# Bias of the second matmul: from TensorE's sums to additions on GpSimd, and a warm-up in small tiles

## The chip, the cores and the metric

The kernel runs on one core of one Trainium2 chip. The core has five engines with queues of their own: TensorE (PE, matmuls, with its weight loads shown apart as PEld), VectorE (DVE), ScalarE (ACT), GpSimd (POOL) and SyncE (SP, which here only issues DMAs). PE writes to PSUM; DVE and ACT read and write PSUM and SBUF; POOL works on SBUF here. The metric is the time of one execution on the device, in microseconds (us); less is better.

## What is computed

```python
xn = layernorm(x)                                   # x: 2048 x 512
s = A(xn)       # a state space layer: a long convolution of each of 512 channels, with its skip
h = gelu(xn @ w1 + b1)                              # 2048 x 1792
g = silu(h @ w2 + b2)                               # 2048 x 512
out = x + s * g
```

The change concerns `+ b2` alone: the same 512 numbers are added to every row of `h @ w2`.

## The kernel before

The rows of xn are cut into four groups of 512 (index t or v, 0 to 3), each of four blocks of 128 rows (index i). The 1792 columns of h are cut into 14 blocks (f). Every operand of the two large products is split into a high and a low part, and three matmuls (high by high, high by low, low by high) stand for one. The weights do not all fit, so the four groups go through the first seven blocks of h (v = 0 to 3), and then again through the other seven (v = 4 to 7). Between the two passes the sums of a group wait in device memory.

For each pair (v, f): `first_half` makes h before its activation in PSUM, `gate` applies the activation on ACT (tile hf), `gate_high` takes the high part (hh, ACT), `ffn_rest` the low part (hl, DVE), and `second_part` adds the three products with the block of w2 to the sums z of the group, four PSUM tiles of 128 x 512, one for each i.

After the seventh block of the first pass, `z_copy(t, i)` empties the sums into SBUF (tile zo): ACT copies the even ones (L411), DVE takes the odd ones and adds b2 while doing so (L413, with b2b, b2 spread over all 128 rows by one DMA, L443). `z_keep` stores zo (SP, L416). In the second pass `z_load` brings them back (zi, L422), DVE's `z_add` adds the new sums (L451), and ACT applies silu. For the last group `z_last` lets ACT copy the sums and POOL add them (L455, L456).

So for odd i, b2 is added by DVE in the copy. For even i it is put into PSUM by PE: in `second_part`, before the first product of a group, one matmul of a 128 x 128 tile of ones with b2r starts the sum (L292). b2r has b2's high part in row 0 and its low part in row 32 and zeros elsewhere; `bias_load`, `bias_high` and `bias_low` make it and the ones, with two DMAs of POOL's queue, two memsets (DVE), two casts (ACT) and a subtraction of one row (DVE). `bias_load` also makes the tile `one`, on which ACT loads its tables early.

Beside all this, the same engines build the convolution's kernel, in 32 steps s: `gen_phase` (PE, a bf16 matmul into one of two PSUM buffers called ph, L620), `gen_round` (ACT L628 or DVE L630), `gen_wrap` (DVE, L634, the last reader of ph), `gen_size` (POOL, tile mm, L640 to L645), `gen_sin` (ACT), `gen_tables` (DVE, tiles e, L666 to L673, from mm and ra, all in SBUF), and for each two steps `gen_sum` (PE, 64 matmuls of 128 x 32 by 128 x 64, L682, two records each) and `gen_out` (ACT, L693). The split of later weights into high and low parts (`split`) is done by ACT and DVE, three times by POOL (L236).

What runs on an engine runs in the order in which the program issues it. That order is written out by hand: ORDER is a list of about 1250 tokens such as `S.16.0` (second_part of pair 16, block 0) or `Z.6` (gen_size of step 6), each of which calls one of the functions above. The tokens that matter here: `O.t.i` z_copy, `OK.t` z_keep, `ZL.t` z_load, `ZA.t.i` z_add, `Z.s` gen_size, `E.s.n` gen_tables, `R.j` ffn_rest, `S.j.i` second_part, `A.s.h` gen_phase, `Q.j` gen_sum, `WS.f.k` split, `KL` table loads on SP, `BL` bias_low.

After the list follow the convolution's transforms, almost all of them matmuls in tiles smaller than the whole array (L895, L911, L965, L1037), to the end.

Before the list the prologue loads the first rows and normalizes them. While it waits, `warm(n)` keeps PE busy with n matmuls of the identity by itself, 128 x 128 in f32, which the profile shows as two records each: 6 of them, a small transpose, then 17 more.

Of the kernel before, what the change touches and what calls it, by code (L numbers as in the profile page):

```python
# [20 lines left out]
P = 128  # L21
# [12 lines left out]
TB = 4  # L34
# [14 lines left out]
W.2 P.0 P.0 WB.2 WS.1.0 WS.1.1 WS.1.2 W.4 W.3 F.1.0 F.1.1 BL G.0 WS.2.0 P.0 LL.2 LL.3 WS.4.0 H.0 WB.3 WS.2.1  # L49
WS.0.3 G.1 WS.2.2 P.0 W.5 F.2.0 WS.3.0 H.1 P.0 R.0 F.2.1 G.2 WB.5 WB.4 WS.5.0 WS.5.1 WS.3.1 WS.2.3 W.6 S.0.0  # L50
WS.4.1 WS.3.2 R.1 F.3.0 WS.4.2 F.3.1 S.0.1 WS.1.3 G.3 S.0.2 H.2 LS.3.1 S.1.0 LS.2.0 LS.3.0 WS.6.0 H.3 LS.2.1
P.0 LD.0 S.1.1 F.4.0 S.1.2 P.0 P.0 F.4.1 P.1 WS.5.2 P.0 P.0 WB.6 LR.2 P.0 CB S.0.3 F.5.0 KL.0.0 KL.1.0 P.0 G.4
R.2 H.4 F.5.1 S.1.3 S.2.0 LD.1 S.2.1 S.2.2 R.3 LL.5 G.5 P.1 LC.2 S.2.3 TF.2.0 LC.3 WS.3.3.1 WS.6.1 WS.4.3.1
TF.2.1 A.0.0 B.0.0 A.0.1 S.3.0 H.5 LL.4 TH.2.0 TL.2.0 S.3.1 S.3.2 R.4 TH.2.1 TF.3.1 P.0 S.3.3 A.1.0 WS.5.3.1
C.0.0 TL.2.1 WS.6.2 KL.2.0 R.5 LD.3 TH.3.1 TL.3.1 S.4.0 B.0.1 C.0.1 F.6.0 WS.6.3 F.6.1 P.0 B.1.0.1 TF.3.0 G.6
KL.0.1 TH.3.0 KL.3.0 H.6 LS.5.0 S.4.1 N.0.0 C.1.0 A.1.1 KL.1.1 S.4.2 Z.0 B.1.1 LS.5.1 TL.3.0 S.5.0 F.8.0 LD.2
LS.4.0 S.5.1 R.6 N.0.1 S.6.0 LS.4.1 A.2.0 Z.1 C.1.1 S.6.1 F.7.0 S.4.3 A.2.1 N.1.0 S.5.2 F.7.1 N.1.1 F.8.1 LR.4
KL.3.1 BB S.5.3 E.0.0 LC.4 S.6.2 G.7 F.9.0 S.6.3 P.1 E.0.1 E.0.2 G.8 E.1.0 F.9.1 LK.0 F.10.0 E.1.1 A.3.0 O.0.0
H.7 R.7 E.1.2 B.2.0.1 TF.4.0 O.0.2 KL.4.0 KL.2.1 F.10.1 H.8 C.2.0 G.9 Q.0 LK.1 B.2.1 R.8 C.2.1 S.7.0 TF.4.1
S.7.1 Z.3 S.7.2 H.9 R.9 B.3.0.1 N.2.0 LD.4 D A.3.1 TH.4.0 KL.4.1 S.8.0 O.0.1 G.10 S.9.0 Z.2 P.1 U.0 N.2.1  # L60
C.3.0 B.3.1 H.10 O.0.3 S.7.3 UD.0 F.11.0 S.8.1 S.9.1 TL.4.0 E.2.0 S.8.2 TH.4.1 P.1 C.3.1 N.3.0 E.2.1 F.11.1
A.4.0 A.4.1 KL.5.0 LC.5 N.3.1 S.9.2 OK.0 KL.6.0 F.12.0 R.10 B.4.0.1 TL.4.1 F.12.1 E.2.2 E.3.0 S.10.0 P.1 B.4.1
LD.5 S.8.3 Z.4 C.4.0 G.12 C.4.1 S.10.1 E.3.1 TF.5.1 P.1 S.9.3 S.10.2 TF.5.0 KL.5.1 E.3.2 G.11 P.1 TH.5.1 Q.1
TH.5.0 LL.7 A.5.0 LL.6 N.4.0 TL.5.1 S.10.3 A.5.1 H.11 B.5.0 U.1 F.13.0 H.12 TL.5.0 F.13.1 P.1 KL.7.0 R.11
F.14.0 C.5.0 R.12 LS.6.0 N.4.1 F.14.1 P.1 S.11.0 P.2 S.12.0 S.11.1 S.11.2 B.5.1 E.4.0 G.13 H.13 P.1 G.14 C.5.1
A.6.0 F.15.0 E.4.1 S.11.3 N.5.0 F.15.1 P.1 N.5.1 KL.7.1 E.4.2 F.16.0 S.12.1 Z.5 S.12.2 H.14 A.6.1 B.6.0.1 R.13
LS.7.0 S.12.3 A.7.0 S.13.0 KL.6.1 S.13.1 S.13.2 LS.7.1 G.15 E.5.0 C.6.0 E.5.1 E.5.2 P.2 B.6.1.1 B.7.0 R.14
H.15 C.7.0 S.13.3 C.6.1 O.1.0 F.16.1 LS.6.1 F.17.0 Z.7 P.1 F.17.1 O.1.2 S.14.0 N.6.0 R.15 LR.6 S.15.0 G.16
# [95 lines left out]
def kernel(  # L164
# [118 lines left out]
    def second_part(v, f, i):  # L283
# [7 lines left out]
        if rows:  # L291
            PE.matmul(z, ones, b2r, start=True, stop=False)  # L292
# [122 lines left out]
    def z_keep(t):  # L415
        SY.dma_start(za[t].rearrange("i p d -> p i d"), zt[t, "o"])  # L416
# [843 lines left out]
```

## Time and profile before

| | |
|---|---|
| median of 3 runs | 524.7 us (524.53 to 524.74) |
| span of the profiled execution, first to last instruction | 523.6 us |
| what lies around the span, by the median of the runs | 1.1 us |
| records of PE matmuls | 5447 |
| instructions of POOL | 425, 329.8 us busy |

The profiled execution has no time of its own beside its span, so the median of the runs stands for it. A row of the timeline reads: start and length in us, engine, line, operation, output<-inputs, shape, count; in brackets the idle time of the engine before it, and what ended it. A row of a line's or a tile's own view has durations in ns (least/median/most), then the first and last start in us. A matmul's length covers its way through the array and overlaps the next one's: what it costs in a full queue is the step from one start to the next.

### The profile page before, as it was taken

Reading aid. Unit: us, or ns where it says so; the run is one execution under the profiler, and the core shown is the slowest. Engines: PE = TensorE matmul, PEld = TensorE weight load, DVE = VectorE, ACT = ScalarE, POOL = GpSimd, SP = SyncE. Lnnn points to the kernel's source line nnn. Section 1 sums busy time; section 2 is a strip of 40 time slices with the busy share of each in tenths; the row PEclk is TensorE's granted clock in tenths of the full one; section 3 lists DMA queues with packets and bytes.
Section 4 is the critical chain, followed back from the end, with each engine's and each line's share of the span. In section 5 each row is a group of like instructions: output and inputs, shape, how many; then the busy total and the mean of one; then the engine's idle time right before and its main releaser. Section 6 shows DMA issues by size and latency. Waiting matters only on the chain.

```text
span 523.6 us, 13568 instructions
## 1 busy us (share of the span) xinstructions
PE 505.3 (97%) x5447; PEld 371.7 (71%) x5447; DVE 456.7 (87%) x698; ACT 357.6 (68%) x518; POOL 329.8 (63%) x425
## 2 busy tenths in 40 slices
PE   7999999999999999999999999999999999999993
PEld 7777777777777777777778777777754565656671
DVE  6999989997889979999999899799767878697885
ACT  4838976788688889968779997888824333334340
POOL 6748598664857397975874845684336433947732
PEclk9999999999999999999999999999999999999998
DMA  8757965239266839150067376148469979364694
GB/s 228 188 160 231 297 177 172 69 98 297 74 174 192 255 121 327 41 201 33 32 172 206 114 205 176 59 71 149 134 199 371 173 170 146 98 147 97 147 241 99
DMA packets 106751, 85.63 MB, mean 164 GB/s; under 512 B 41646, under 2 KB 82624, under 8 KB 106688
## 3 DMA queue, kind: packets, MB, share of 16 engines
q1 hardware_dynamic: 96400, 65.80, 48.4%
q0 software_dynamic: 8960, 17.97, 11.4%
q10 hardware_dynamic: 1328, 0.98, 0.7%
q8 instruction: 43, 0.70, 0.6%
q14 instruction: 20, 0.16, 0.1%
HBM read 51.18 MB, written 33.55 MB: 162 GB/s over the span
## 4 chain that ended last, share of the span: by engine, by line
PE 70%; DVE 17%; ACT 4%; POOL 2%; issue 2%; DMA 2%; SPq 0%; ACTq 0%; POOLq 0%; DVEq 0%
PE s L911 12%; PE z L293 7%; PE z L294 7%; PE z L295 7%; PE f L251 7%; PE f L253 7%; PE f L252 7%; PE sa_p L965 6%; PE kg L682 4%; PE s L895 3%; DMA x<-in_A_u_dram 2%; PE ph L620 2%; DVE hl L280 2%; DVE x L368 2%; DVE e L670 1%
## 5 line engine op out<-in xcount | busy, mean ns | idle before, releaser
L643 POOL TENSOR_TENSOR mm<-mm,rc 128x32 f32<-128x32 f32 (+4 forms) x150 | 108.1, 721 | 11.8
L293 PE MATMUL z<-w2h,hh 128*128 128x512 f32 x224 | 97.7, 436 | 0.0
L251 PE MATMUL f<-xh,w1h 128*128 128x512 f32 x220 | 90.5, 411 | 1.0 <-DVE xl L400 1.0
L295 PE MATMUL z<-w2h,hl 128*128 128x512 f32 x224 | 88.4, 395 | 0.8 <-DVE hl L280 0.8
L294 PE MATMUL z<-w2l,hh 128*128 128x512 f32 x224 | 88.6, 396 | 0.0
L252 PE MATMUL f<-xl,w1h 128*128 128x512 f32 x220 | 86.9, 395 | 0.8 <-DVE xl L400 0.8
L253 PE MATMUL f<-xh,w1l 128*128 128x512 f32 x220 | 86.9, 395 | 0.4 <-DVE w1l L236 0.4
L911 PE MATMUL s<-X,mc 128*64 128x256 f32 x512 | 64.2, 393 | 0.4 <-DVE X L903 0.4
L640 POOL COPY mm<-rc 128x32 f32<-128x32 f32 x30 | 19.5, 652 | 64.9 <-DVE e L673 42.6
L930 DVE TENSOR_TENSOR t<-s,uh 128x512 f32<-128x512 f32 x62 | 39.7, 669 | 20.8 <-ACT uh L922 20.8
L911 PEld LDWEIGHTS s<-X,mc 128*64 128x64 f32 x512 | 34.1, 134 | 31.6 <-issue 5.9
L666 DVE TENSOR_TENSOR e<-mm,ra 128x1024 f32<-128x1024 f32 x32 | 43.6, 1366 | 13.6 <-ACT ra L654 8.7
L268 ACT ACTIVATE hf<-f,b1s 128x512 f32<-128x512 f32 x56 | 38.1, 689 | 19.5 <-PE f L253 11.6
L293 PEld LDWEIGHTS z<-w2h,hh 128*128 128x128 f32 x224 | 42.5, 190 | 12.7 <-issue 3.9
L280 DVE TENSOR_TENSOR hl<-hf,hh 128x512 fp32r<-128x512 f32 x56 | 49.5, 890 | 2.1 <-ACT hh L274 2.0
L922 ACT COPY uh<-s 128x512 f32<-128x512 f32 x31 | 18.2, 586 | 48.5 <-PE s L911 35.4
L295 PEld LDWEIGHTS z<-w2h,hl 128*128 128x128 f32 x224 | 42.1, 188 | 11.3 <-DVE hl L280 1.2
L251 PEld LDWEIGHTS f<-xh,w1h 128*128 128x128 f32 x220 | 41.5, 188 | 10.8 <-DVE xl L400 1.3
L253 PEld LDWEIGHTS f<-xh,w1l 128*128 128x128 f32 x220 | 41.3, 188 | 10.7 <-DVE w1l L236 0.8
L252 PEld LDWEIGHTS f<-xl,w1h 128*128 128x128 f32 x220 | 41.3, 188 | 10.5 <-DVE xl L400 1.2
L294 PEld LDWEIGHTS z<-w2l,hh 128*128 128x128 f32 x224 | 42.3, 189 | 8.3
L634 DVE SCALAR_TENSOR_TENSOR ra<-ra,ph 128x512 f32<-128x512 f32 x64 | 42.9, 679 | 5.1 <-ACT ra L628 4.5
(204 smaller groups left out, 1085.5 us busy)
## 6 DMA issues: line engine op xcount, KB each, us to landing
xs<-x SPq DMA_DIRECT2D x16, 256.0 KB
xt_h<-xh POOLq DMA_DIRECT2D x4, 1024.0 KB, 6.4
xt_l<-xl POOLq DMA_DIRECT2D x4, 1024.0 KB, 8.6
kgd<-ko SPq DMA_DIRECT2D x16, 256.0 KB
za<-zo SPq DMA_DIRECT2D x4, 1024.0 KB
xh<-xt_h POOLq DMA_DIRECT2D x4, 1024.0 KB, 6.6
xl<-xt_l POOLq DMA_DIRECT2D x4, 1024.0 KB, 9.2
zi<-za SPq DMA_DIRECT2D x4, 1024.0 KB
```

What stands on the lines that cost most here:

```text
L251: PE.matmul(p, wh[:, k, :], xh[:, k, :], start=(k == 0), stop=False)
L252: PE.matmul(p, wh[:, k, :], xl[:, k, :], start=False, stop=False)
L253: PE.matmul(p, wl[:, k, :], xh[:, k, :], start=False, stop=(k == KD - 1))
L280: V.tensor_sub(hl, hf, hh)
L293: PE.matmul(z, hh[:, s], wh, start=(f0 == 0 and not rows), stop=False)
L294: PE.matmul(z, hh[:, s], wl, start=False, stop=False)
L295: PE.matmul(z, hl[:, s], wh, start=False, stop=(f0 == FA - 1))
L634: V.scalar_tensor_tensor(ra[:, 0, c], ra[:, 1, c], MAGIC, p, op0=ALU.subtract, op1=ALU.subtract)
L643: GP.tensor_mul(mv[:, :, 0:3:2, w:2 * w], mv[:, :, 0:3:2, 0:w], rc[:, 2 + 2 * i:4 + 2 * i, :].rearrange("p j c -> p c j").unsqueeze(3).to_ ...
L666: V.tensor_mul(e1, m1.unsqueeze(1).to_broadcast([P, 2, CH, N1]), ra[:, :, :, :N1])
L911: PE.matmul(p[ka * 64:(ka + 1) * 64, o], SB["mc"][:, 2 * k + jj, o, :], xf[b][:, k, :, :, jj], start=True, stop=True, skip_group_check=True)
L930: V.tensor_mul(sm[b, g // 2][i][:, :, 2 * (g % 2):2 * (g % 2) + 2], p[:, :, i, 1].unsqueeze(1).to_broadcast([P, 2, 2, P]), uh)
```

## The change

PE no longer puts b2 into the even sums. ACT copies them to SBUF as before, and POOL adds b2b to the copy there: for groups 1 and 2 between the copy and its store (`OB`), for groups 0 and 3 after the sums have come back for the second pass (`ZB`). The stores of groups 1 and 2 come later in the order. b2r, the ones and what made them are gone; the tile `one` is kept for the early table load. In the warm-up, 17 full matmuls become 5 full ones and then 116 small ones, in tiles of 64 x 32, 32 x 128 and 32 x 32 of the array, with 64 or 128 columns moving, the last two groups with strided operands.

```diff
-        rows = f == 0 and i % 2 == 0
-        if rows:
-            PE.matmul(z, ones, b2r, start=True, stop=False)
-        PE.matmul(z, hh[:, s], wh, start=(f0 == 0 and not rows), stop=False)
+        PE.matmul(z, hh[:, s], wh, start=(f0 == 0), stop=False)
...
+    def z_bias(z, i):
+        GP.tensor_add(z[:, i, :], z[:, i, :], b2b)
...
-    def bias_load():
-        SB["b2"] = st = wka.tile([P, TB * P], F32, tag="hf", name="b2st", bufs=2)
-        V.memset(st, 0.0)
-        for k in (0, 32):
-            GP.dma_start(st[k:k + 1], b2.rearrange("(o d) -> o d", o=1))
-        one = wka.tile([P, TB * P], F32, tag="hf", name="one", bufs=2)
-        V.memset(one[:, :P], 1.0)
+    def tables_first():
+        SB["one"] = one = wka.tile([P, TB * P], F32, tag="hf", name="one", bufs=2)
+        V.memset(one[:, :1], 1.0)
         A.activation(one[:, P:P + 1], one[:, :1], AF.Sqrt)
-        A.copy(ones, one[:, :P])
-        SB["one"] = one
-
-    def bias_high():
-        A.copy(b2r, SB["b2"])
-
-    def bias_low():
-        V.tensor_sub(b2r[32:33], SB["b2"][32:33], b2r[32:33])
...
+    def warm_tiles():
+        ps = [ps1.tile([P, D], F32, tag="z", name=f"wt{i}", bufs=TB) for i in range(4)]
+
+        def one(r, q, w, n, k, cs=1, ms=1):
+            rows, cols = slice(r * k, r * k + k), slice(q * w, q * w + w)
+            x = ident.unsqueeze(1).to_broadcast([P, 2, P])[rows] if n == 2 * P else ident[rows, 0:n * ms:ms]
+            PE.matmul(ps[r][cols, :n], ident[rows, 0:w * cs:cs], x, start=True, stop=True, skip_group_check=True)
+
+        for w, n, k, turns, cs, ms in ((32, 64, 64, 3, 1, 1), (32, 128, 64, 2, 1, 1), (P, 64, 32, 3, 1, 1), (32, 64, 32, 2, 1, 1),
+                                       (32, 64, 64, 2, 4, 1), (32, 64, 64, 2, 1, 2)):
+            for _ in range(turns):
+                for q in range(P // w):
+                    for r in range(P // k):
+                        one(r, q, w, n, k, cs, ms)
...
-        bias_load()
+        tables_first()
         warm(6)
         next(step)
-        warm(17)
+        warm(5)
+        warm_tiles()
...
-        bias_high()
...
-        "BL": bias_low,
+        "OB": lambda t, i: z_bias(zt[t, "o"], i),
+        "ZB": lambda t, i: z_bias(fin[t], i),
```

The order, where its tokens differ (the tokens on both sides stand for the place):

```text
before                                  after
F.1.1 BL G.0                            F.1.1 G.0
S.16.0 Z.6 LC.7                         S.16.0 Z.6 OB.1.0 OB.1.2 LC.7
S.17.1 OK.1 E.7.0                       S.17.1 E.7.0
F.20.0 KL.9.0 F.20.1                    F.20.0 KL.9.0 OK.1 F.20.1
WB.10 OK.2 WS.8.1                       WB.10 WS.8.1
S.24.0 WS.8.2.1 G.26                    S.24.0 WS.8.2.1 OB.2.0 OB.2.2 OK.2 G.26
C.17.0 Z.19                             C.17.0 ZB.0.0 ZB.0.2 Z.19
UD.13 ZL.3 ST                           UD.13 ZL.3 ZB.3.0 ZB.3.2 ST
```

More of the change, by code (lines that the diff above doesn't have):

```diff
@@ L54 @@
[L54 to L68, printed above, removed]
@@ new lines @@
+S.18.1 P.2 TH.7.0.1 A.9.1 KL.10.0 UD.2 R.19 Q.3 B.9.1 TL.7.1 N.8.0 S.18.2 C.9.1 U.3 TL.7.0 P.2 F.22.0 A.10.0 F.22.1
+W.12 KL.10.1 Z.9 Z.8 S.18.3 N.8.1 S.19.0 KL.11.0 N.9.0 G.22 N.9.1 S.19.1 F.21.0 E.8.0 LD.7 R.20 S.19.2 S.20.0 E.8.1
+WB.8 B.10.0.1 XL.0 O.2.0 P.2 E.8.2 F.21.1 KL.11.1 S.20.1 F.23.0 A.10.1 G.21 W.9 B.10.1 H.21 Z.10 UD.3 E.9.0 C.10.0
+LD.6 E.9.1 A.11.0 S.19.3 S.20.2 E.9.2 F.23.1 C.10.1 B.11.0.1 H.22 R.21 F.25.0 N.10.0 A.11.1 C.11.0 W.7 WS.8.0 R.22
+S.20.3 Q.4 G.23 N.10.1 KL.12.0 F.25.1 B.11.1.1 S.21.0 H.23 C.11.1 F.24.0 O.2.2 O.2.3 O.2.1 F.24.1 S.22.0 N.11.0 N.11.1
@@ new lines @@
+S.25.2 A.14.1 WB.12 S.25.3 H.27 E.12.0 S.26.1 Z.13 R.27 N.13.0 N.13.1 U.5 G.28 WS.10.1 W.11 S.27.0 E.12.1 WS.12.0
+S.26.2 F.29.0 S.26.3 KL.15.1 H.28 UD.5 E.12.2 E.13.0 F.30.0 O.3.0 P.2 XL.1 F.29.1 A.15.0 G.29 WS.10.2.1 E.13.1 WS.13.0
+B.14.0 WB.13 S.27.1 S.27.2 E.13.2 C.14.0 WS.12.1 B.15.0.1 WB.11 B.14.1.1 WS.9.3.1 C.14.1 WS.13.1 R.28 S.27.3 WS.8.3
+F.30.1 H.29 P.2 F.31.0 WS.11.0 KL.18.0 Q.6 S.28.0 KL.16.1 G.30 C.15.0 WS.11.1 A.15.1 WS.13.2 WS.12.2 S.28.1 O.3.1
+N.14.0 WS.11.2 R.29 Z.14 O.3.3 S.29.0 Z.15 P.3 S.28.2 B.15.1.1 F.33.0 O.3.2 F.31.1 S.29.1 A.16.0 WS.10.3 N.14.1 U.6
@@ new lines @@
+F.33.1 H.30 S.28.3 C.15.1 A.16.1 KL.17.0 OK.3 S.29.2 N.15.0 E.14.0 N.15.1 UD.6 KL.17.1 F.32.0 G.31 ZL.0 KL.19.0
+WS.12.3.1 WS.11.3.1 E.14.1 E.14.2 B.16.0 H.31 F.32.1 R.30 S.30.0 Z.16 S.29.3 G.33 C.16.0 G.32 F.34.0 B.16.1.1 S.30.1
+R.31 E.15.0 C.16.1 A.17.0 S.31.0 N.16.0 E.15.1 E.15.2 A.17.1 S.30.2 Z.17 S.30.3 P.3 H.32 B.17.0 N.16.1 KL.19.1 Q.7
+H.33 S.31.1 C.17.0 ZB.0.0 ZB.0.2 Z.19 S.31.2 F.34.1 KL.21.0 B.17.1.1 S.31.3 U.7 C.17.1 N.17.0 A.18.0 R.32 F.35.0
+WS.13.3 E.16.0 G.34 A.18.1 E.16.1 R.33 E.16.2 B.18.0 S.32.0 C.18.0 H.34 F.36.0 F.35.1 SC KL.18.1 N.17.1 UD.7 F.36.1
@@ new lines @@
+N.20.1 P.3 S.36.2 B.21.0 A.21.1 F.41.1 R.38 Z.20 ZD.0 C.21.0 F.40.1 S.37.1 S.37.2 S.36.3 B.21.1 H.39 S.38.0 P.3 C.21.1
+S.38.1 Z.21 Q.9 P.3 G.41 P.3 S.37.3 G.40 S.38.2 R.39 N.21.0 H.40 S.39.0 KL.23.1 N.21.1 E.20.0 Z.22 S.39.1 F.43.0
+E.20.1 F.42.0 R.40 A.22.0 U.9 E.20.2 S.38.3 P.3 E.21.0 S.39.2 E.21.1 Z.23 F.42.1 ZL.1 S.40.0 UD.9 A.22.1 B.22.0.1
+E.21.2 C.22.0 F.43.1 H.41 P.3 S.40.1 G.42 S.39.3 B.22.1 A.23.0 R.41 C.22.1 H.42 S.40.2 B.23.0 S.41.0 S.41.1 KL.24.0
+S.41.2 A.23.1 P.3 Q.10 KL.24.1 N.22.0 SL1.2 C.23.0 ZA.1.0 ZA.1.2 R.42 S.40.3 KL.25.0 G.43 F.44.0 N.22.1 B.23.1.1
@@ new lines @@
+C.23.1 U.10 XL.3 E.22.0 F.44.1 A.24.0 KL.25.1 KL.27.0 Z.24 E.22.1 S.42.0 H.43 S.41.3 F.45.0 E.22.2 ZA.1.1 N.23.0 R.43
+N.23.1 F.45.1 S.43.0 A.24.1 G.44 F.46.0 B.24.0 S.42.1 UD.10 G.45 C.24.0 A.25.0 S.42.2 A.25.1 F.47.0 S.42.3 H.44 ZA.1.3
+E.23.0 B.24.1.1 C.24.1 E.23.1 ZG.1 KL.26.0 E.23.2 R.44 F.47.1 B.25.0 C.25.0 S.44.0 N.24.0 B.25.1 S.43.1 SL1.1 Q.11
+H.45 S.44.1 KL.26.1 ZD.1 S.43.2 C.25.1 N.24.1 R.45 S.45.0 A.26.0 S.45.1 S.43.3 Z.25 KL.27.1 E.24.0 N.25.0 N.25.1
+S.44.2 E.24.1 U.11 ZL.2 B.26.0.1 F.46.1 E.24.2 G.46 S.44.3 S.45.2 G.47 E.25.0 A.26.1 B.26.1 A.27.0 F.48.0 C.26.0
@@ new lines @@
+E.28.1 F.52.1 F.53.0 N.29.1 S.49.1 ZA.2.1 G.51 A.31.0 H.51 U.13 ZA.2.2 S.50.0 S.49.2 E.29.0 G.52 E.28.2 E.29.1 A.30.0
+KL.31.1 E.29.2 B.31.0 R.51 F.55.0 S.49.3 F.53.1 S.51.0 B.30.0 ZG.2 A.30.1 C.31.0 S.50.1 C.30.0 S.50.2 H.52 B.30.1.1
+SL1.3 Z.31 Z.30 A.31.1 G.53 C.30.1 S.50.3 Q.14 N.30.0 N.30.1 F.55.1 R.52 B.31.1.1 C.31.1 N.31.0 E.30.0 N.31.1 F.54.0
+S.51.1 E.30.1 S.51.2 ZD.2 G.55 S.52.0 S.52.1 E.30.2 E.31.0 E.31.1 S.52.2 S.51.3 UD.13 ZL.3 ZB.3.0 ZB.3.2 ST F.54.1
+E.31.2 H.53 U.14 R.53 UD.14 S.52.3 KL0 H.55 R.55 G.54 H.54 Q.15 U.15 R.54 UD.15
@@ L700 @@
     cbs = par.tile([CH * NPC, CH * NPH], BF16, name="cbs")
-    b2r = wka.tile([P, D], F32R, name="b2r")
-    ones = wka.tile([P, P], F32R, name="ones")
     b2b = wka.tile([P, D], F32, name="b2b")
```

96 lines of the change are left out of this document (38 added, 58 removed).

## The prediction

> **What bounds the kernel now.** I read the page first: its span, its busy line and its chain by engine.
>
> ```profile
> span 523.6 us, 13568 instructions
> PE 505.3 (97%) x5447; PEld 371.7 (71%) x5447; DVE 456.7 (87%) x698; ACT 357.6 (68%) x518; POOL 329.8 (63%) x425
> PE 70%; DVE 17%; ACT 4%; POOL 2%; issue 2%; DMA 2%; SPq 0%; ACTq 0%; POOLq 0%; DVEq 0%
> ```
>
> TensorE (PE) is nearly full, GpSimd (POOL) has 37% free: moving work from one to the other looks like a plain gain. But 17% of the chain lies on VectorE (DVE). So the next view is the busy time by stretch (its columns: length, then PE, weight loads, DVE, ACT, POOL, granted clock, DMA share, GB/s).
>
> ```profile
> 24.00:97.00 73.00, 69.58 (x552) 53.97 (x551) 69.99 (x133) 54.35 (x84) 55.26 (x77) 1.00 0.66 194
> 97.00:147.00 50.00, 50.00 (x357) 39.21 (x361) 44.74 (x79) 38.90 (x60) 31.77 (x47) 1.00 0.43 131
> 210.00:258.00 48.00, 47.24 (x531) 36.65 (x534) 46.48 (x57) 39.17 (x48) 36.36 (x47) 1.00 0.22 74
> 258.00:382.00 124.00, 124.00 (x1414) 96.46 (x1402) 110.58 (x145) 107.23 (x132) 74.54 (x97) 1.00 0.55 140
> 396.00:506.00 110.00, 109.97 (x1550) 66.35 (x1548) 87.67 (x131) 38.41 (x70) 64.38 (x57) 1.00 0.77 169
> ```
>
> In 24 to 97 and in 210 to 258 DVE is as full as PE; in the others PE alone is. Who waits for whom at the seams is in the timeline:
>
> ```profile
> 96.83 0.50 PE L251 MATMUL f<-xh,w1h 128*128 128x512 f32 x1 [1.03 <-DVE xl L400]
> 143.70 0.69 DVE L630 TENSOR_SCALAR ra<-ph 128x512 f32<-128x512 f32 x1 [1.72 <-PE ph L620]
> 183.72 0.69 DVE L280 TENSOR_TENSOR hl<-hf,hh 128x512 fp32r<-128x512 f32 x1 [0.53 <-ACT hh L274]
> 257.93 1.36 DVE L666 TENSOR_TENSOR e<-mm,ra 128x1024 f32<-128x1024 f32 x1 [0.69 <-PE kg L682]
> ```
>
> At 96.83 PE waits for DVE; at 143.70 DVE waits for PE. So time saved on PE counts between 97 and 147 and after, but not before 97, where DVE sets the pace.
>
> **What the change removes.** Eight matmuls:
>
> ```profile
> L292 PE MATMUL z<-b2r,ones x8: 388/396/499, 21.4 to 177.2; 128*128 128x512 f32 x8
> 120.22 0.40 PE L292 MATMUL z<-b2r,ones 128*128 128x512 f32 x1
> 127.70 0.40 PE L292 MATMUL z<-b2r,ones 128*128 128x512 f32 x1
> 127.94 0.39 PE L293 MATMUL z<-w2h,hh 128*128 128x512 f32 x1
> ```
>
> Their ends overlap the next one; the step from 127.70 to 127.94 is what one costs, 0.24, so 1.9 for eight. They come as two for each of the first four groups of sums. The first four lie before 97: they only lengthen PE's wait at 96.83, and I count them at nothing (at most 0.9 if DVE's pace there were not the bound). Those at 120.22 and 127.70 and the last, at 177.2, give 0.7. The seventh lies in 147 to 177, where the chain of waits goes over ACT and DVE: nothing. **Gain: 0.7.**
>
> Also gone are two small DMAs on POOL's queue, a memset and a one-row subtraction on DVE, and two ScalarE casts, all in the first steps (below, with the warm-up).
>
> **What it adds.** Eight POOL additions of 128x512, four pairs. The nearest operation in kind and shape is already there; beside it stand two POOL subtractions of the same shape, and what DVE did meanwhile:
>
> ```profile
> L456 POOL TENSOR_TENSOR zi<-zl,zi x4: 1287/1292/1296, 389.7 to 396.1; 128x512 f32<-128x512 f32 x4
> 219.90 2.27 POOL L236 TENSOR_TENSOR w2l<-w2s,w2h 128x512 fp32r<-128x512 f32 x1
> 222.13 1.74 POOL L236 TENSOR_TENSOR w2l<-ws,w2h 128x512 fp32r<-128x512 f32 x1
> 220.94 1.78 DVE L672 TENSOR_TENSOR e<-mm,ra 128x512 f32<-128x512 f32 x1
> 222.64 1.77 DVE L673 SCALAR_TENSOR_TENSOR e<-mm,ra 128x512 f32<-128x512 f32 x1
> 378.12 0.69 DVE L673 SCALAR_TENSOR_TENSOR e<-mm,ra 128x512 f32<-128x512 f32 x1
> 123.62 1.28 DVE L413 TENSOR_TENSOR zo<-z,b2b 128x512 f32<-128x512 f32 x2
> 123.77 1.05 POOL L645 TENSOR_TENSOR mm<-mm,rc 128x512 f32<-128x512 f32 x1
> ```
>
> An addition takes 1.29 when nothing is in its way, 10.3 in all. The four rows at 220 are the heart of this prediction: POOL and DVE, both with two operands in SBUF, do not run together but take turns. L673 takes 0.69 alone (378.12) and 1.77 there; two POOL operations delayed DVE by 2 x 1.08 = **2.2 per pair**. When DVE reads one operand from PSUM (L413 at 123.62: two in 1.28 beside POOL's 1.05) neither is held up. So each new pair costs DVE between 0 and 2.6 (twice 1.29); I take 2.2, since the rows at 220 are the same pattern. POOL itself has gaps for all four pairs. What counts is what DVE does in each gap, and how much room PE has behind it.
>
> Pair 1 (sums 1) stands behind POOL's group that ends at 124.82:
>
> ```profile
> 131.61 0.78 POOL L545 TENSOR_TENSOR pr_m<-pr_bi 128x128 f32<-128x128 f32 x1 [6.79 <-DVE pr_bi L539]
> 125.41 1.00 DVE L368 TENSOR_SCALAR x<-x,mv,rs 128x512 f32<-128x512 f32 x2
> 126.99 1.23 DVE L666 TENSOR_TENSOR e<-mm,ra 128x1024 f32<-128x1024 f32 x1 [0.58 <-ACT ra L654]
> ```
>
> POOL is idle to 131.61: hidden there. DVE loses 2.2, less the 0.58 it waits anyway: 1.6 late at 126.99. At 143.70 it was 1.72 ahead of PE; with 1.6 lost and PE 0.5 earlier it is 0.4 behind. So PE pays 0 to 0.4; I take **0.2**.
>
> Pair 2 (sums 2) stands behind the L236 at 173.08:
>
> ```profile
> 173.08 1.35 POOL L236 TENSOR_TENSOR w1l<-w1s,w1h 128x512 fp32r<-128x512 f32 x1
> 183.11 0.24 POOL L640 COPY mm<-rc 128x32 f32<-128x32 f32 x1 [8.68 <-DMA rc<-recd]
> 187.05 0.69 DVE L634 SCALAR_TENSOR_TENSOR ra<-ra,ph 128x512 f32<-128x512 f32 x1
> 189.10 0.38 PE L620 MATMUL ph<-cbs,lh 96*128 96x512 bf16 x1
> ```
>
> POOL has until 183.11. DVE is 2.2 late, 1.7 after its 0.53 wait at 183.72. The L634 at 187.05 frees one of the two PSUM buffers of ph, and the L620 at 189.10 takes it 1.36 after its end. PE comes 0.24 earlier, so it stalls 1.7 - 1.36 + 0.24 = **0.6** (0 to 1.0), and everything behind PE's queue with it.
>
> Pair 3 (final sums 0) waits for its load and for POOL's L645, which ends at 238.15:
>
> ```profile
> 236.77 1.38 POOL L645 TENSOR_TENSOR mm<-mm,rc 128x512 f32<-128x512 f32 x1
> 250.30 0.68 DVE L280 TENSOR_TENSOR hl<-hf,hh 128x512 fp32r<-128x512 f32 x1
> 251.23 0.40 PE L295 MATMUL z<-w2h,hl 128*128 128x512 f32 x1
> ```
>
> Here DVE builds tables from SBUF (L666 to L673) and has no wait until 257.93. The hl that ends at 250.98 is read at 251.23, a room of 0.25: PE stalls 2.2 - 0.25 = **1.95** (0 to 2.35).
>
> Pair 4 (final sums 3) waits for a load of 1 MB. In the windows its traffic ends near 372.8; POOL is free by then, DVE is in the last tables:
>
> ```profile
> 368.60:372.80 4.20, 4.20 (x112) 3.57 (x102) 1.58 (x2) 4.16 (x5) 2.45 (x3) 1.00 0.78 254
> 379.17 1.99 PE L682 MATMUL kg<-e,e 128*32 128x64 f32 x128
> ```
>
> The last table ends with the L673 of 378.12, at 378.81; PE's L682 at 379.17 reads it, 0.36 later. PE stalls 2.2 - 0.36 = **1.85** (0 to 2.25), and from there to 506 PE is full, so it reaches the end.
>
> The stores of sums 1 and 2 move behind pairs 1 and 2 on SyncE's queue, past one and two table loads there, which now go first. I count that at nothing, since nothing on PE's path reads them before the final loads:
>
> ```profile
> L422 SPq DMA_DIRECT2D zi<-za x4: 370/374/377, 230.2 to 367.7; - x4
> ```
>
> If a store were so late that the next copy into its buffer waited, ScalarE would stand still behind it; the copies are tens of us apart, so I see no price there.
>
> **The start.** 17 full-size warm matmuls become 5 and 116 small ones (232 records, two for each):
>
> ```profile
> 6.11 4.74 PE L448 MATMUL warm<-ident 128*128 128x128 f32 x34
> 124.98 1.99 PE L682 MATMUL kg<-e,e 128*32 128x64 f32 x128
> 18.95 0.29 DVE L533 TENSOR_TENSOR pr_ci<-pr_bi,pr_cr 128x128 f32<-128x128 f32 x1 [0.69 <-DMA x<-in_A_u_dram]
> ```
>
> The 24 records removed are 24 x 0.14 = 3.3. The nearest small tiles, L682, take 1.99/128 = 0.0155 each: 232 are 3.6, and changes of tile shape may add some. DVE idles 0.69 at 18.95 and loses a subtraction before it: I take **0**, between -0.4 (DVE starts earlier) and +1.3 (the small ones take up to twice that row's time, less the wait and the subtraction). The Trainium skill, TensorE: Matmul & The Clock Gate, section "Wait — 56ns, not 53.3ns?", says that starts of matmuls never come closer than about 25 ns; 232 x 0.025 would be 5.8, an estimate by that page, and would put the sum near the upper end. This case's L682 row shows 15.5 ns, so the row decides.
>
> **Sum.** -0.7 + 0.2 + 0.6 + 1.95 + 1.85 + 0 = +3.9. The profiled span of 523.6 becomes 527.5; the runs' median of 524.7 stands 1.1 above the span (launch and end), so I predict 528.6. A measurement of this kernel can tell about 0.2%, 1.05 us, from no change.
>
> **Rivals.**
> 1. *The turns cost PE nothing* (chance 0.2). The mechanism: POOL gets the port only while DVE reads PSUM or waits, as at 123.62, so DVE's 250.30 and 378.12 come less than 0.25 and 0.36 late; below that point only the gain is left. 524.7 - 0.7 = 524.0, down to 523.6 with the start. For it: POOL's own gaps are wide everywhere. Against it: at 220 POOL got its turn after each DVE operation.
> 2. *One of pairs 3 and 4 is paid* (0.2). Pair 4 depends on when a load lands; an addition done before 371 or after 379 meets no tables. 528.6 - 1.9 = 526.7.
> 3. *The warm-up is long as well* (0.1): +1.3 on the forecast, 529.9; or the clock falls back after weak work. The window 396 to 506 is small and half-size tiles at a granted clock of 1.00, against it.
> 4. *The change doesn't do what it says*: eight matmuls are removed by line, so no chance of its own.
>
> The forecast itself has 0.5; alone it reaches from 527.3 to 530.3. Chances: slower by over 0.2% 0.76 (forecast, rivals 2 and 3, less a little of 2), same 0.14, faster 0.10 (rival 1 split). The range from 523.9 to 530.5 leaves out some of rival 1 and the bounds' far ends.
>
> **What would show it.** After: L236-like rows of the new additions near 1.3 to 2.5 on POOL; DVE's L666 to L673 beside pairs 3 and 4 at 1.8 and more; a wait of PE at the hl near 250 and at the last L682, each near 2; the warm-up ending within 1 of 10.85 (6.11 + 4.74). Wrong if DVE's rows there keep their 0.7 and 1.2, or if PE's two waits are absent.

## The result, and the profile after

The changed kernel takes 536.3 us (median of 5 runs, 534.7 to 537.2) against 524.5 for the kernel before on the same chip (524.4 to 524.7): the ratio is 1.0221, with a 95% interval of 1.0205 to 1.0237. It is slower, as forecast, but by 11.8 us where 3.9 was predicted, and outside the range. The profiled execution took 537.0, its span is 535.2.

The page of the changed kernel (span, PE's busy line, the chain by engine):

```profile
span 535.2 us, 13976 instructions
PE 509.7 (95%) x5647; PEld 373.1 (70%) x5647; DVE 464.1 (87%) x696; ACT 356.7 (67%) x516; POOL 346.1 (65%) x431
PE 57%; DVE 27%; ACT 6%; issue 5%; POOL 4%; DMA 1%; POOLq 0%; DVEq 0%; ACTq 0%
```

PE is busy for 4.4 us longer (505.3 before), though eight large matmuls are gone, and its share of the span falls; in the chain DVE rises from 17 to 27%, and "issue" from 2 to 5%. Issue is time in which an engine waited for nothing that the profile shows. Line numbers shift with the edits: hl, L280 before, is L275 here, and the sums of L682 are L680. The view of PE's waits (total in us, times, longest) names both:

```profile
PE z L287 <- DVE hl L275: 3.0, 2, 2.4
PE wt L439 <- issue: 2.4, 1, 2.4
PE s L892 <- issue: 1.7, 1, 1.7
...
PE kg L680 <- DVE e L671: 0.8, 1, 0.8
...
PE z L286 <- issue: 0.7, 1, 0.7
```

To see where the time is lost for good, I take matmuls that both kernels have and subtract the start in the trace of before from the start in the trace of the other kernel. This lag, at some places (us in the span of before), stands in this table for the changed kernel and the kernels of the experiments below:

```text
place            100    170    240    256    322    356    379    384    514
after          +2.86  +2.47  +2.39  +6.49  +7.43  +7.65  +7.59 +11.96 +12.03
big_warm       -2.07  -2.08  -1.93  +0.71  +0.71  +0.71  +0.70  +2.30  +2.35
no_final_adds  +3.80  +3.39  +3.03  +3.53  +4.57  +4.84  +4.79  +9.04  +9.11
tiles_alone    +3.19  +3.19  +3.20  +3.20  +4.29  +7.97  +7.92  +8.75  +8.74
tiles_80       -0.41  -0.61  -0.46  +3.57  +3.57  +3.57  +3.55  +5.24  +5.30
tiles_144      +1.44  +0.80  +0.96  +5.08  +5.08  +5.08  +5.08  +6.68  +6.73
no_adds        -2.05  -2.48  -2.72  -2.74  -2.73  -2.73  -2.74  -2.74  -2.69
adds_late      -0.72  -0.93  -0.79  -0.35  +0.30  +0.30  +0.28  +0.28  +0.61
pages_shift    -0.37  -0.78  -1.16  -0.74  +1.06  +1.06  +1.06  +6.49  +6.59
mixed_a        -0.52  -1.19  -2.32  -1.88  -1.71  -1.71  -1.40  -1.02  -0.98
```

The changed kernel is 2.9 late at 100. It loses 4.1 between 240 and 256, 0.9 before 322, and 4.4 between 379 and 384. (Up to 100 the lag also differs by some 1.6 between executions of the same code: tiles_80 and no_adds are alike there. And each row is one execution, which can lie off its kernel's median: those of big_warm and tiles_80 took 527.4 and 530.3, the fastest and the slowest of their six.) The four places, one after the other.

**The start.** The timeline of the changed kernel, PE in the warm-up (the small matmuls write to wt), and the windows around it (length, PE, weight loads, DVE, ACT, POOL, granted clock, DMA share, GB/s):

```profile
7.73 3.23 PE L439 MATMUL wt<-ident 64*32 64x64 f32 x200
13.39 0.56 PE L439 MATMUL wt<-ident 64*32 64x64 f32 x32 [2.43 <-issue]
13.88 3.48 PE L377 MATMUL xT<-ident,x 128*128 128x128 f32 x16
```

```profile
10.00:13.40 3.40, 0.97 (x78) 0.74 (x65) 3.01 (x9) 1.79 (x3) 2.80 (x8) 1.00 0.81 192
13.40:16.80 3.40, 3.40 (x46) 3.23 (x47) 0.99 (x2) 1.24 (x3) 3.06 (x9) 0.53 0.92 256
16.80:18.00 1.20, 1.20 (x11) 1.20 (x10) 1.04 (x2) 1.12 (x3) 0.00 (x0) 0.90 0.82 177
```

200 of the 232 small records run in 3.23 us, 16 ns each. Then PE stands still for 2.43 us, waiting for nothing that is shown, and runs the last 32. The transposes, which began at 10.68 before, begin at 13.88 and run at half clock (0.53).

**240 to 256.** POOL's additions to the final sums 0, two of DVE's rows beside them, and PE's wait behind; then the clock:

```profile
241.61 4.51 POOL L408 TENSOR_TENSOR zi<-zi,b2b 128x512 f32<-128x512 f32 x2
242.66 2.31 DVE L668 TENSOR_TENSOR e<-mm,ra 128x1024 f32<-128x1024 f32 x1
244.89 1.78 DVE L275 TENSOR_TENSOR hl<-hf,hh 128x512 fp32r<-128x512 f32 x1
256.13 0.80 PE L287 MATMUL z<-w2h,hl 128*128 128x512 f32 x1 [2.36 <-DVE hl L275]
```

```profile
254.00:256.00 2.00, 0.00 (x0) 0.00 (x0) 2.00 (x3) 0.00 (x0) 0.78 (x2) 0.99 0.00 0
256.00:258.00 2.00, 1.86 (x4) 1.31 (x5) 1.93 (x7) 0.58 (x1) 1.69 (x5) 0.50 0.03 8
```

The two DVE rows are 1.1 longer each than those of their kind that no POOL operation meets (0.68 for the hl, as at 250.30 before). That is the 2.2 of the prediction, and PE waits 2.36. Behind the wait PE has half its clock, which costs another 1.5.

**379 to 384.** The additions to the final sums 3 and the same pattern, and then, at another place, a wait without a cause:

```profile
380.76 3.81 POOL L408 TENSOR_TENSOR zi<-zi,b2b 128x512 f32<-128x512 f32 x2 [2.01 <-DMA zi<-za]
381.63 1.79 DVE L670 TENSOR_TENSOR e<-mm,ra 128x512 f32<-128x512 f32 x1
383.34 1.78 DVE L671 SCALAR_TENSOR_TENSOR e<-mm,ra 128x512 f32<-128x512 f32 x1
...
388.65 1.10 PE L680 MATMUL kg<-e,e 128*32 128x64 f32 x64 [0.80 <-DVE e L671]
```

```profile
394.02 1.06 PE L892 MATMUL s<-raw,fc 32*32 32x512 f32 x7 [1.75 <-issue]
```

**322.** A short wait of the same sort: the row below. What these three have in common is seen in the DMA view. Instructions come to the core through queues of their own. q8 is taken for PE's, by the count: it moved 44 packets (the page; 0.72 MB, so 16 KB each, for 2 x 5647 matmuls and weight loads, about 257 a packet). One of them falls between 391.5 and 392.6, none else from 390.0 to the end of the wait. The rows are the wait near 322, the queue of the whole span, and the queue from 391.5 to 392.6:

```profile
327.93 0.50 PE L286 MATMUL z<-w2l,hh 128*128 128x512 f32 x1 [0.65 <-issue]
```

```profile
q8 instruction: 44, 0.72, 0.6%
```

```profile
q8 instruction: 1, 0.02, 5.3%
```

In the start, a packet falls between 10.6 and the 13.39 at which PE goes on. That PE ran out of instructions was a guess at this point; the experiments test it.

### The profile page after: what moved, and what is told of

Read it like the earlier page. It is cut to its first block, busy times and chain, and to the rows that moved or that the text cites. A ratio compares the mean times of both kernels' runs of the same rounds, so it can differ in the third digit from the quotient of the medians.

```text
span 535.2 us, 13976 instructions
## 1 busy us (share of the span) xinstructions
PE 509.7 (95%) x5647; PEld 373.1 (70%) x5647; DVE 464.1 (87%) x696; ACT 356.7 (67%) x516; POOL 346.1 (65%) x431
## 4 chain that ended last, share of the span: by engine, by line
PE 57%; DVE 27%; ACT 6%; issue 5%; POOL 4%; DMA 1%; POOLq 0%; DVEq 0%; ACTq 0%
PE s L908 10%; PE sa_p L962 5%; PE z L285 5%; PE z L287 5%; PE z L286 5%; PE f L246 5%; PE f L247 4%; PE f L248 4%; DVE e L668 4%; PE kg L680 3%; PE s L892 3%; DVE hl L275 3%; DVE e L671 2%; DVE e L664 2%; DVE ra L632 2%
## 5 line engine op out<-in xcount | busy, mean ns | idle before, releaser
L641 POOL TENSOR_TENSOR mm<-mm,rc 128x32 f32<-128x32 f32 (+4 forms) x150 | 112.3, 749 | 11.8
L275 DVE TENSOR_TENSOR hl<-hf,hh 128x512 fp32r<-128x512 f32 x56 | 50.1, 900 | 1.3 <-ACT hh L269 1.3
```

The costliest lines, as they stand in the source:

```text
L275: V.tensor_sub(hl, hf, hh)
L641: GP.tensor_mul(mv[:, :, 0:3:2, w:2 * w], mv[:, :, 0:3:2, 0:w], rc[:, 2 + 2 * i:4 + 2 * i, :].rearrange("p j c -> p c j").unsqueeze(3).to_ ...
```

## The experiments

Beside each of the four sets of experiments ran the kernel before on the same chip: its medians were 524.45, 524.24, 524.38 and 524.50. Intervals are 95%.

**The old warm-up with the new additions (big_warm).**

```diff
-        warm(5)
-        warm_tiles()
+        warm(17)
```

> The changed kernel with the old second part of the warm-up: 17 full matmuls instead of 5 and 116 small ones. Theory A (PE runs out of instructions where small tiles follow each other: it idled 2.43 us at 13.39 in the warm-up, 0.65 at 327.93 and 1.75 at 394.02, each ending 1.3 to 1.6 us after a 16 KB packet of the instruction queue): the stall of 13.39 goes, and since 416 PE instructions fewer stand ahead, the ends of the 16 KB pieces fall elsewhere, so the two later ones go as well: about 536.3 - 3.1 - 3.2 = 530.0. Rival B (the stall of 394.02 follows from the late additions to sums 3, that of 327.93 is chance): only the start is regained, 533.2. Rival C (the start is made up by 235 us and costs nothing at the end): 536.3.

Measured: 529.9 (527.4 to 530.5), ratio 1.0101 [1.0084, 1.0117]. That is theory A's 530.0: the start and both later waits without a cause are gone, and what is left are the additions, 2.6 between 240 and 256 and 1.6 at 384 in the table. But the table's execution took 527.4, with the clock at 1.00 behind the wait for hl (shown below); the other five took 529.3 to 530.5, at a lower mean clock, and have no trace.

**No additions to the final sums 0 and 3 (no_final_adds).** In the order:

```diff
-ZB.0.0 ZB.0.2
...
-ZB.3.0 ZB.3.2
```

> The changed kernel without the four POOL additions to the final sums 0 and 3 (the even blocks of these two groups are left without b2). Theory A (POOL and DVE take turns; the stall before the hl of pair 34 was 2.36 us and long enough for the clock to fall for some 1.5 us more; sums 3 cost 0.8 to 1.4): 536.3 - 4.1 - 1.2 = 531.0, with the granted clock at 1.00 in 235 to 258, and the stalls of the instruction pieces near 328 and 391 to 394 still there. Rival B (the stall at 394 comes from sums 3 being late): 527.9, that stall gone too. Rival C (the additions are not what delays DVE): over 535.

Measured: 534.2 (533.2 to 534.3), 1.0182 [1.0169, 1.0195]. The wait near 254 and the low clock are gone (1.00 from 235 to 258), and the wait in the transforms is still there, so that it isn't the late sums 3 that cause it; rival B falls:

```profile
391.10 0.63 PE L894 MATMUL s<-raw,fc 32*32 32x512 f32 x4 [2.43 <-issue]
```

But 2.1 was saved and not 5.3. By the table this execution was 0.9 later at 100, lost 0.6 between 256 and 300, where the changed kernel lost nothing, and its wait in the transforms was longer (2.43 for 1.75). The 0.6 is such a wait, too: 0.31 at 262.37. And between 379 and 384 it loses 4.25, where the changed kernel, with the additions to the sums 3, loses 4.37: their delay and the wait for instructions overlap, so that leaving out the additions saves next to nothing there.

**The new warm-up alone (tiles_alone).** The kernel before with `warm(5)` and `warm_tiles()`.

> The kernel before with the new warm-up alone (5 full matmuls and 116 small ones; b2 still added by PE). Theory A (instruction pieces): the stall near 13.4 and half clock after it, worth 3.1 at the end, and the pieces end 416 instructions later, within 16 of where they end in the changed kernel, so stalls near 326 and 382 too, up to 3.2: 527.6 to 530.8. Rival B (the warm-up costs its own length alone, as predicted): 524.3 to 526.0. Rival C (made up by 235 us): 524.5.

Measured: 533.8 (530.8 to 534.2), 1.0161 [1.0138, 1.0185]. Four fifths of the loss are there with the warm-up alone, though nothing behind it is changed; the shares of warm-up and additions don't add up, since the later waits shift. Rivals B and C fall. A wait without a cause comes at 358.80 this time, and the clock falls behind it, which the expectation had not counted; this one place costs 3.7 in the table:

```profile
358.80 0.50 PE L252 MATMUL f<-xl,w1h 128*128 128x512 f32 x1 [1.86 <-issue]
...
361.94 0.63 PE L252 MATMUL f<-xl,w1h 128*128 128x512 f32 x1
```

```profile
361.00:363.00 2.00, 2.00 (x6) 1.52 (x5) 2.00 (x4) 0.00 (x0) 0.00 (x0) 0.50 1.10 116
```

**80 small matmuls, and 144 (tiles_80, tiles_144).** The first shortens the list in `warm_tiles`, the second raises the turns of one form:

```diff
 tiles_80
-(P, 64, 32, 3, 1, 1), (32, 64, 32, 2, 1, 1), (32, 64, 64, 2, 4, 1), (32, 64, 64, 2, 1, 2)
+(P, 64, 32, 2, 1, 1), (32, 64, 32, 2, 1, 1)
 tiles_144
-(P, 64, 32, 3, 1, 1)
+(P, 64, 32, 10, 1, 1)
```

> The changed kernel with 80 small matmuls in the warm-up instead of 116: 144 PE instructions fewer, so that from the warm-up on the 16 KB pieces (256 instructions) end where they do in the kernel before. Theory A: no stall near 328 and 394 (-3.2); and fewer small tiles follow each other in the start, where the piece now ends among the transposes: the stall of 2.43 goes in part or whole (up to -3.1): 530.0 to 533.1. Rival B (the small tiles cost by their number): 536.3 - 0.5 = 535.8.

> The changed kernel with 144 small matmuls in the warm-up instead of 116: PE's 16 KB pieces of instructions end, after the warm-up, where they do with 80 and in the kernel before, but the small tiles are more. Theory A (position of the pieces): the stall at the 224th matmul, near 13.4, stays with the half clock after it (3.1), those at the 3019th and 3783rd go (3.2): 533.1 to 534.0. Rival B (cost by the number of small tiles: 116 cost 536.3, 80 cost 527.4): 540 or more. Rival C (the later stalls were chance): 536.3 to 537.

Measured: 527.4 (526.9 to 530.3), 1.0070 [1.0052, 1.0089], with 80, and 532.3 (531.2 to 535.9), 1.0168 [1.0139, 1.0197], with 144. Neither has a wait without a cause at 322 or in the transforms. With 80 the start has none either; with 144 it comes at the same matmul as with 116 (223 matmuls ahead), half as long: there the 200 in front took 4.26 us and not 3.23. The rows are of tiles_80 (two) and tiles_144:

```profile
8.04 2.57 PE L439 MATMUL wt<-ident 64*32 64x64 f32 x160
10.87 2.11 PE L377 MATMUL xT<-ident,x 128*128 128x128 f32 x16 [0.26 <-DVE x L360]
```

```profile
14.06 1.15 PE L439 MATMUL wt<-ident 32*32 32x64 f32 x84 [1.26 <-issue]
```

More small tiles than the change has, and less time: cost by their number (rival B of tiles_144) falls; the 532.3 is 0.8 under the range of theory A. The 80 came out better than expected, as the whole start was regained.

**The later waits without the rest (pages_shift).** From a kernel without late waits (adds_late, below), 36 small matmuls more where PE waits for DVE anyway, so that as many PE instructions stand ahead of the later stages as in the changed kernel:

```diff
+    def warm_more():
+        p = ps1.tile([P, D], F32, tag="f1", name="wm", bufs=2)
+        for n in range(36):
+            r, q = 0, n % 4
+            PE.matmul(p[q * 32:q * 32 + 32, r * 64:r * 64 + 64], ident[r * 32:r * 32 + 32, 0:32], ident[r * 32:r * 32 + 32, 0:64],
+                      start=True, stop=True, skip_group_check=True)
...
-F.8.0
+WM F.8.0
```

> The kernel with 80 small matmuls and late additions, with 36 more small matmuls into a PSUM tile that nobody reads, ahead of the first matmuls of the second group near 96, where PE waits 1.1 us for DVE anyway: 144 PE instructions more, so that from there on the 16 KB pieces end where they do in the changed kernel, with neither its start nor its early additions. Theory A (position of the pieces): stalls near 326 and at 380 to 390, each some 2.2 to 2.8 us after a packet of the instruction queue, together 2 to 4: 526.7 to 528.7. Rival B (the stalls of the changed kernel came from its lateness, not from the pieces): 524.6 to 525.2 and no such stall.

Measured: 529.4 (528.4 to 532.6), 1.0108 [1.0084, 1.0132]: 4.7 more than without the 36, which themselves cost nothing (-0.37 at 100 in the table, where the start varies by more). There are waits without a cause of 0.86 at 258.65 and 0.39 at 321.56, and the one in the transforms is back:

```profile
387.01 1.75 PE L903 MATMUL s<-raw,fc 32*32 32x512 f32 x7 [2.12 <-issue]
```

And it is at the same matmul. The windows count PE's matmuls from the start of the span to the wait (length, PE busy with the count, clock, DMA share, GB/s); here for the changed kernel, no_final_adds, tiles_alone and pages_shift:

```profile
0.00:327.90 327.90, 314.40 (x3019) 0.99 0.58 167
0.00:394.00 394.00, 377.95 (x3783) 0.99 0.56 158
```

```profile
0.00:325.00 325.00, 313.16 (x3019) 0.99 0.58 168
0.00:391.05 391.05, 376.72 (x3783) 1.00 0.56 159
```

```profile
0.00:324.30 324.30, 314.07 (x3019) 0.99 0.58 168
0.00:358.75 358.75, 346.71 (x3402) 1.00 0.55 160
```

```profile
0.00:321.50 321.50, 312.74 (x3019) 1.00 0.59 170
0.00:387.00 387.00, 375.86 (x3783) 1.00 0.56 161
```

The times differ by up to 7 us, the counts not at all, but for the second of tiles_alone: 3402 is 381 before 3783, nearly three pieces of 128 matmuls with their loads, so that it is the end of another piece. And as tiles_alone still has the eight matmuls of b2, its wait at the count of 3019 is before another matmul of the program. So it is the position in PE's stream of instructions that decides where such a wait can come. Not whether: tiles_alone passes 3783, in the same transforms, without one, and the changed kernel 3402 (0.22 lost); 2383, at which pages_shift waits 0.86 and no_final_adds 0.31, costs the changed kernel nothing.

The traces tie the end of the waits to the packets. Six kernels have such waits of 0.3 us and more, 14 in all, 0.31 to 2.90 long; each ends 2.2 to 2.8 us after a packet of this queue began and 1.2 to 1.6 after it ended. (Not every "issue" is of this sort: the 0.84 before a transpose near 45 has no packet, and the kernel before has it too.)

**One addition of pair 3 instead of two (one_add_early).** From tiles_80:

```diff
-ZB.0.0 ZB.0.2
+ZB.0.0
...
-ZA.0.3
+ZA.0.3 ZB.0.2
```

> The kernel with 80 small matmuls, and of the pair of additions to the final sums 0 only the first at its place; the second stands behind the last of DVE's additions to these sums (near 274), where PE has 2.9 us of room before the next hl. Theory A (each addition makes DVE 1.1 to 1.2 late; the clock falls only after the longer stall): the stall near 253 is 1.2 instead of 2.40 and the granted clock stays 1.00 behind it in every run: 527.3 - 1.2 = 526.1, no run over 527.5. Rival B (the delay does not go by the number of additions): stall and time as with two, 527.3 with some runs at 530.3.

Measured: 526.7 (525.6 to 527.2), 1.0041 [1.0028, 1.0055]. The wait is 1.05, with full clock, and no run took over 527.2: theory A, if 0.6 over its 526.1. Below the row of this kernel; then that of tiles_80 with its window, and that of big_warm with its own:

```profile
249.98 0.50 PE L289 MATMUL z<-w2h,hl 128*128 128x512 f32 x1 [1.05 <-DVE hl L277]
```

```profile
253.32 0.79 PE L287 MATMUL z<-w2h,hl 128*128 128x512 f32 x1 [2.40 <-DVE hl L275]
```

```profile
253.00:255.00 2.00, 1.68 (x4) 1.19 (x5) 1.97 (x6) 0.39 (x1) 1.71 (x4) 0.50 0.03 8
```

```profile
251.82 0.51 PE L287 MATMUL z<-w2h,hl 128*128 128x512 f32 x1 [2.36 <-DVE hl L275]
```

```profile
252.00:254.00 2.00, 2.00 (x9) 1.53 (x10) 1.93 (x6) 1.38 (x2) 1.76 (x4) 1.00 0.03 8
```

After 2.40 the clock is 0.50, after 2.36 in another execution it is 1.00. A wait of this length can cost the clock and need not.

**Pair 3 on DVE itself (dve_pair3).** From tiles_80, `V.tensor_add` for group 0 at the place of the change.

> The kernel with 80 small matmuls, where the two additions to the final sums 0 stand at the place of the change, but run on DVE itself instead of POOL. Theory A (an addition on POOL takes 1.1 from DVE beside its tables; on DVE it takes 0.69, the least row of such an operation): PE's stall near 253 is 1.4 to 1.6 instead of 2.40, no half clock behind it: 526.3 to 526.8. Rival B (POOL takes the work off DVE at least in part): stall 2.4 or more, 527.4 and up to 530.3.

Measured: 526.8 (526.2 to 529.7), 1.0056 [1.0037, 1.0074], and the waits are smaller though DVE does the work itself:

```profile
234.03 1.78 DVE L408 TENSOR_TENSOR zi<-zi,b2b 128x512 f32<-128x512 f32 x2
234.16 1.99 PE L679 MATMUL kg<-e,e 128*32 128x64 f32 x128 [1.36 <-DVE ra L631]
...
251.38 0.50 PE L287 MATMUL z<-w2h,hl 128*128 128x512 f32 x1 [0.62 <-DVE hl L275]
```

PE waits 0.62 near 251, and 0.6 more than the 0.76 of before at 234. The two additions take 1.78 of DVE; on POOL they took 2.2 from it. Theory A holds in the size of the time, with the wait in two parts; one of the six runs took 529.7 at a lower mean clock (0.992), which it had not expected.

**Additions late, and none (adds_late, no_adds).** From tiles_80; adds_late puts pair 3 behind DVE's last addition to these sums, and pair 4 into `z_last`, ahead of POOL's own:

```diff
-ZB.0.0 ZB.0.2
...
-ZA.0.3
+ZA.0.3 ZB.0.0 ZB.0.2
...
-ZB.3.0 ZB.3.2
...
+        if i % 2 == 0:
+            z_bias(fin[t], i)
         GP.tensor_add(fin[t][:, i, :], z, fin[t][:, i, :])
```

> The kernel with 80 small matmuls, with both additions to the final sums 0 behind DVE's last addition to them (near 274) and those to the final sums 3 directly ahead of POOL's additions to them (392 and 395), where DVE reads PSUM. Theory A (turns of POOL and DVE cost only where PE waits for DVE within 2.2 us): no stall near 253 (-2.5, and -1.5 for the clock) and none near 385 (-1.3): 522.0 to 524.0. Rival B (eight additions on POOL cost wherever they stand): over 526.

> The kernel with 80 small matmuls and none of the eight POOL additions (the even blocks of all groups are left without b2): what the eight removed matmuls are worth by themselves. Theory A: 524.5 - 0.7 - up to 0.4 of the start = 523.4 to 523.9; equal within 0.5 to the kernel whose additions stand late. Rival B (the matmuls were hidden): 524.5.

Measured: 524.7 (523.6 to 525.7), 1.0009 [1.0000, 1.0018], late, and 522.7 (522.3 to 523.7), 0.9976 [0.9966, 0.9986], with none, which leaves b2 out of all even blocks. The waits near 253 and 385 are gone, but late additions still cost 2.0 against none, more than expected. In the table the removed matmuls are worth 0.64 from 100 on (-2.05 to -2.69); what is left of the 1.5 by which no_adds is faster would lie in the start, which varies by as much.

**All pairs late (pool_late, dve_late).** As adds_late, with the pairs of groups 1 and 2 also behind DVE's last addition to their final sums (`ZA.1.3`, `ZA.2.2`); in dve_late those of groups 0 to 2 run on DVE.

> The kernel with 80 small matmuls, with all four pairs late and on POOL: those of groups 0 to 2 behind DVE's last addition to the final sums of the group, those of group 3 ahead of POOL's own. Theory A: the stall of 0.82 near 189 goes with pair 2, some 0.7 at 275 and as much or less at 313 and 361 take its place: 523.8 to 525.0. Rival B (free at these places): 522.7.

> The same, but the late pairs of groups 0 to 2 on DVE instead of POOL (1.2 to 1.4 us of DVE for each pair, where PE has 1.6 to 3 us of room before the next hl). Theory A (DVE loses less by doing an addition than by taking turns with POOL): 522.7 to 523.6, faster than the kernel before (524.2) by the value of the removed matmuls, and not slower than the one with the late pairs on POOL. Rival B (POOL is the cheaper place): slower than that by 0.5 or more.

Measured: 526.4 (526.3 to 527.6), 1.0045 [1.0033, 1.0057], on POOL, 525.7 (524.9 to 526.4), 1.0027 [1.0018, 1.0036], on DVE. Both expectations were too low. DVE comes out 0.7 better, but that doesn't show it to be the better place: pool_late has a wait without a cause that dve_late has not, 0.75 in the lag. It stands 127 matmuls, one piece, behind the 3402 of tiles_alone:

```profile
375.39 0.50 PE L288 MATMUL z<-w2l,hh 128*128 128x512 f32 x1 [0.59 <-issue]
```

The one large wait of dve_late stands behind pair 1 of the change, that of group 1, whose two additions take DVE 2.84 here:

```profile
307.85 2.84 DVE L410 TENSOR_TENSOR zi<-zi,b2b 128x512 f32<-128x512 f32 x2
313.21 0.39 PE L621 MATMUL ph<-cbs,lh 96*128 96x512 bf16 x1 [1.66 <-DVE ra L635]
```

**Each pair at its place (mixed_a, mixed_b).** Group 1 on POOL as in the change, groups 0 and 2 late on DVE, group 3 in `z_last`; in mixed_b group 2 as in the change, too.

> The kernel with 80 small matmuls, the additions of group 1 on POOL at the place of the change, those of groups 0 and 2 late and on DVE, those of group 3 ahead of POOL's own. With all of groups 0 to 2 late on DVE the one large stall was 1.66 at 313, behind the pair of group 1. Theory A (a pair costs only where its own place has no room): that stall goes and no other comes: 525.7 - 1.7 = 524.0, down to 523.0. Rival B (DVE or PE pays for each pair somewhere): 525 or more.

> The same with the additions of group 2 on POOL at the place of the change, too. Theory A: a stall of 0.8 near 189 comes, which PE's wait near 234 takes back: within 0.5 of the kernel above. Rival B: slower than it by 0.8.

Measured: 523.8 (522.4 to 524.9), 0.9986 [0.9976, 0.9996], and 524.3 (522.7 to 524.8), 0.9994 [0.9983, 1.0005]. mixed_a is as theory A had it, and 0.14% faster than the kernel before, at the edge of what its interval can tell. Pair 2 at the place of the change costs 0.6 by the medians, between its two theories, and the two intervals overlap.

## Why the prediction was wrong

- **The removed matmuls, -0.7: right.** 0.64 from 100 on, without the additions.
- **Pair 1, +0.2: nothing in the changed kernel.** Lag 2.47 at 130 and at 170 (tiles_80 loses 0.6 from 130 to 150 and has regained 0.5 by 170).
- **Pair 2, +0.6: right at its place.** In the changed kernel the lag rises by 0.56 at 190 and by 0.42 more at 208; the wait that PE had at 234.77 before gives 0.82 back. "Everything behind PE's queue with it" was the part that was wrong: a delay is lost only up to the next wait behind it.
- **Pair 3, +1.95: the mechanism right, the price low.** DVE's delay was 2.2, the wait 2.36 to 2.40, the lag 2.6 with full clock (big_warm). The missing term is the clock: 1.5 more in the changed kernel. The text looked for a falling clock after weak work only, not after a wait that it had itself forecast.
- **Pair 4, +1.85: near.** 1.6 in big_warm, and as much in the changed kernel up to the wait at 394.02; DVE's L670 and L671 grew by 1.1 each as forecast. PE's wait at the last sums was 0.80, though, not near 2; the rest came in small steps behind it.
- **The start, 0 (-0.4 to +1.3): the step that failed.** It priced the small tiles by the time of one record, and that was right: 16 ns measured for 15.5 taken, not the 25 of the Trainium skill (TensorE: Matmul & The Clock Gate, section "Wait — 56ns, not 53.3ns?"). What it left out is that PE must also be fed: 232 such records, each with its weight load, are nearly two 16 KB pieces of instructions, and PE stood still after 200. The warm-up ended at 13.95, 3.1 past the 10.85 of the sign. At 240 the changed kernel is 2.9 later than tiles_80 and 4.3 later than big_warm.
- **A term that is missing altogether.** The longer warm-up moves the ends of all later pieces. In the changed kernel two fall among small tiles or right behind them, and PE stands still 0.65 and 1.75: 1.1 and about 2.8 in the lag (0.92 before 322 and 0.22 by 356; 4.4 between 379 and 384, less the 1.6 of pair 4).

With start 2.4 (at 240, the matmuls and pairs 1 and 2 in it), pair 3 2.6, clock 1.5, pieces 3.9 and pair 4 1.6 the sum is 12.0, the lag at the end. That splits the loss in the order in which it came; without pair 4 the piece at its place costs as much as both (no_final_adds). Of the rivals, the third (the long warm-up, or a clock that falls back) named two of the right things, each too small and for another reason; the second and the first did not happen.

What the runs show is the position, by count, and that PE goes on a nearly fixed time after a packet of its instruction queue, whatever the length of the wait. The Trainium skill, Runtime: NRT & Kernel Launch, section "Instruction fetch mechanics", tells of blocks of 16 KiB and 256 instructions that the engine fetches while it works on the one before, mostly hidden. The trace agrees on the size (16 KB, about 257). Hidden it is at most places, and not always among small tiles: of the 128 matmuls ahead of each of the 14 waits 100 or more are small (at 16 ns, 128 last 2 us), but so are 108 ahead of the 3783 that tiles_alone passes. At which instruction a fetch is asked for was not tried. Nor was it tried in which executions the clock falls; and the 1.5 by which the start varies is in every median here.

## What to carry to other kernels

A change that adds or removes many small instructions on an engine is not local: it moves the engine's pieces of instructions, and where one ends among tiles of 16 ns, or just behind them, the engine can stand still for up to 3 us. Look for "issue" in the waits at the same count of instructions, and try some instructions more or less. An idle second engine is no free place for additions in SBUF: here POOL took 1.1 from DVE for each one that DVE did in 0.9 at the same place (1.4 at 307.85 in dve_late). And a wait that is forecast to be some 2 us long must be priced with the clock that may fall behind it.

## What the runs showed of the hardware

The granted clock fell to 0.50 after waits of PE of 1.86 (tiles_alone), 2.12 (pages_shift), 2.36 (the changed kernel) and 2.40 us (tiles_80), and stayed at 1.00 after 1.75 (the changed kernel, at 394.02), 2.36 (big_warm) and even 2.43 (no_final_adds, at 391.10); so the length of the wait alone doesn't decide it. In the changed kernel it came back at 259.4, and had cost 1.5. The Trainium skill, TensorE: Matmul & The Clock Gate, section "Why this matters for your kernels", advises no idle gaps over about 3 us: here less was enough at times. Half the clock shows in the timeline, too: a row of 128x512 takes 0.63 instead of 0.40.
